# Products of alpha over four pairs of heads: one scan per direction instead of four, and no table A for the first five tiles

## The chip, the cores and the metric

The kernel runs on one core of a Trainium2 chip. The metric is the device time of one execution in microseconds; the median of several runs counts.

## The reference

Three layers follow one another; in what follows 4 batches, 8 heads, 768 positions and heads of 48 are meant.

```python
# 1. gated linear attention, position by position
state = alpha[:, :, t, :, None] * state + einsum('bhd,bhe->bhde', k[:, :, t], v[:, :, t])
y[:, :, t] = einsum('bhd,bhde->bhe', q[:, :, t], state)
# 2. x = y with the heads joined: 3072 rows of 384
xn = x / sqrt(mean(x*x) + 1e-6) * rms_g
x  = (silu(xn @ w_gate) * (xn @ w_val)) @ w_out          # 384 -> 1536 -> 384
# 3. each row to its best of 8 experts: relu(x @ w1[e]) @ w2[e], 384 -> 1024 -> 384,
#    times the gate's probability and a sigmoid of x @ w_output_gate[:, e]
```

The weights of layer 2 come as 64-bit numbers. alpha lies between 0.8 and 1.

## The kernel before

**Tiles.** The 3072 rows are 24 tiles of 128 positions of one batch; three tiles make a group of 384 rows, the unit of layer 2. The heads stand in four pairs (NP = 4): in a tile, the partitions hold the two heads of a pair (at 0 and at 64) and the free dimension holds pair and position, 4 x 128.

**Attention of a tile.** The step-by-step state becomes products of alpha within a tile. Z holds, for each position, the product of alpha over the positions after it; the product over the whole tile is `en`; A holds the product up to the position, divided by `en`. k is multiplied by Z, q by A; then the tile's scores, masked, and the state carried from the tile before give y. Z comes from `after_scan` (L269), a running product that goes backwards along the 127 positions of one pair, A from `upto_scan` (L283), a running product forwards over 128 positions that begins with the reciprocal of `en` (`ends`, L275). Both run on VectorE once per pair, so four times per tile. Their second operand is a column of ones that is broadcast.

**Two ways to bring in a tile.** Tiles 0 to 4 (`prework_nat`, L290) are loaded with positions on partitions and turned by TensorE (L246) into PSUM; the scans read alpha from PSUM, Z lies in a tile named aT, A in a tile named A, and q and k are multiplied on their way out of PSUM, or, by the letters in QM and KM, first copied out by ScalarE and then multiplied by VectorE (v) or GpSimd (p). Tiles 5 to 23 (`prework`, L330) are turned by VectorE (L342) from blocks of SBUF; alpha lies in aT, which the forward scan overwrites with A, and Z lies in a tile named A, of which there are two. Both multiplications (L371) run on VectorE in these tiles.

**Other work on the same engines.** Layer 2's weights arrive as pairs of 32-bit words; VectorE makes floats of them in three steps (L499, L502, L505) and ScalarE (L518) and VectorE or GpSimd (L509) split them in a high and a low part. Layer 2 is three matrix products per block of 128 hidden columns: ps_g and ps_v (L574), with ScalarE's L565 and L588 and VectorE's L566, L585 and L595 (GpSimd for some blocks of the first group) on what they leave in PSUM, and ps_o (L609). Layer 2 of one group runs while the attention of the next groups is prepared.

**What sets the order.** The program order comes from a list written by hand for the first three tiles (START), then from loops that give out one stage of attention or a few preparation steps per block of layer 2. From that order and its own idea of every instruction's cost a planner makes the order on each engine; it may move an instruction ahead of others. `pace` keeps the instructions whose names stand in K0, K1 or K2 in program order among themselves; the scans are named sc and the tile's number (sc0, sc1, sc4 and sc5 occur). SEATS names the PSUM bank of each early product. SIDE puts some tensors of tiles 1 and 2 where late weights will lie. Each engine works off its own queue in order.

Of the kernel before, what the change touches and what calls it, by code (L numbers as in the profile page):

```python
# [8 lines left out]
F32 = mybir.dt.float32  # L9
# [4 lines left out]
ALU = mybir.AluOpType  # L14
# [21 lines left out]
    'CR': [3, 3, 3, 2],  # L36
    'PRN': [1, 2, 1, 1],
    'JS': 6,
    'ABUF': 2,
    'ZBUF': 1,  # L40
    'IB': 0,
    'RA0': 2,
    'RB0': 13,
# [12 lines left out]
def gla_glu_moe_kernel(  # L56
# [16 lines left out]
    nc = tc.nc  # L73
    P = 128
    B, H, S, D = q.shape
    NT, DM = out.shape
    NP = H // 2
# [110 lines left out]
    for i in range(BS):  # L188
        t_ = att.tile([P, NP, 2 * D], F32, name=f"state{i}")
        nc.gpsimd.memset(t_, 0.0)  # L190
        state_of.append(t_)

    vt = {}
    pre = {}
    xT = {}
# [58 lines left out]
    def seat_of(t, nm, shape, bufs=1):  # L254
        if (t, nm) in SIDE:
# [7 lines left out]
    SIDE = {(2, "A"): ("wgle", 0), (2, "qT"): ("wgle", 1), (2, "kT"): ("wgle", 2),  # L263
            (1, "aT"): ("wvhe", 0), (1, "P0"): ("wvhe", 1), (1, "P1"): ("wvhe", 2),
            (1, "kn"): ("wghe", 0), (1, "xn"): ("wghe", 1), (2, "v"): ("wghe", 2)}

    def after_scan(Z, al, p):  # L269

        pace('sc' + str(now[0]), nc.vector.tensor_tensor_scan(out=Z[:, p, P - 2::-1], data0=al[:, p, P - 1:0:-1],
                                                data1=ones_f.to_broadcast([P, P - 1]),
                                                initial=1.0, op0=ALU.mult, op1=ALU.mult))

    def ends(t, Z, al):  # L275

        en = att.tile([P, NP, 1], F32, tag="en", name="en", bufs=4)
        rc = att.tile([P, NP, 1], F32, tag="rc", name="rc", bufs=2)
        pace('sc' + str(now[0]), nc.vector.tensor_tensor(out=en, in0=al[:, :, 0:1], in1=Z[:, :, 0:1], op=ALU.mult))
        pace('sc' + str(now[0]), nc.vector.reciprocal(out=rc, in_=en))  # L280
        return en, rc

    def upto_scan(A, al, rc, p):  # L283

        pace('sc' + str(now[0]), nc.vector.tensor_tensor_scan(out=A[:, p, :], data0=al[:, p, :], data1=ones_f.to_broadcast([P, P]),
                                                initial=rc[:, p, :], op0=ALU.mult, op1=ALU.mult))

    QM, KM, PM, XM, SM, HG, LV = (CFG[x] for x in ("QM", "KM", "PM", "XM", "SM", "HG", "LV"))

    def prework_nat(t):  # L290
        Z = seat_of(t, "aT", [P, NP, P], CFG["ZBUF"])
        A = seat_of(t, "A", [P, NP, P], CFG["ABUF"])
        qT = seat_of(t, "qT", [P, NP, P], 2)
        kT = seat_of(t, "kT", [P, NP, P], 2)
        nc.gpsimd.memset(Z[:, :, P - 1:P], 1.0)
        ps = {}

        def turn_a():
            now[0] = t
            ps[0] = turn_nat(t, 0)  # L300
            for p in range(NP):
                after_scan(Z, ps[0], p)
            en, ps["rc"] = ends(t, Z, ps[0])
            pre[t] = (en, qT, kT)

        def up():
            now[0] = t
            for p in range(NP):
                upto_scan(A, ps[0], ps["rc"], p)

        def turn(x, dst, by, mode):
            def go():
                ps[x] = turn_nat(t, x)
                if mode == "d":
                    pace(f'dm{t}', nc.vector.tensor_tensor(out=dst, in0=ps[x], in1=by, op=ALU.mult))
                else:
                    nc.scalar.activation(dst, ps[x], AF.Copy)
                    pace(f'qm{t}', (nc.gpsimd if mode == "p" else nc.vector).tensor_tensor(out=dst, in0=dst, in1=by, op=ALU.mult))
                if x == 2 and t + 1 == NAT:
                    load_tile(NAT)  # L320
            return go
        return {"a": turn_a, "r": up, "k": turn(1, kT, Z, KM[t]), "q": turn(2, qT, A, QM[t])}

    def load_v(t):
        b, c = place_of[t]
# [4 lines left out]
    def prework(t):  # L330
        if t < NAT:
# [1 line left out]
            for x in CFG['NO']:  # L333
                yield w[x]
            return
        aT = att.tile([P, NP, P], F32, tag="aT", name="aT", bufs=CFG["ZBUF"])
        Z = att.tile([P, NP, P], F32, tag="A", name="Z", bufs=CFG["ABUF"])
        qT = att.tile([P, NP, P], F32, tag="qT", name="qT", bufs=2)
        kT = att.tile([P, NP, P], F32, tag="kT", name="kT", bufs=2)

# [19 lines left out]
        def en():  # L360
            e_, ps["rc"] = ends(t, Z, aT)
            pre[t] = (e_, qT, kT)
        ps = {}
        yield en
        for p in range(0, NP, 2):
            def up(p=p):
                for pp in (p, p + 1):
                    upto_scan(aT, aT, ps["rc"], pp)
            yield up
# [949 lines left out]
```

## Time and profile before

| | |
|---|---|
| time, median of 3 runs | 900.53 us (900.36 to 902.38) |
| the profiled execution, its own time | 900.19 us |
| its span, first to last instruction | 898.5 us |
| TensorE busy with matmuls | 863.2 us (96% of the span) |
| VectorE busy | 579.6 us (65%) |
| ScalarE busy | 278.2 us (31%) |
| GpSimd busy | 197.3 us (22%) |
[...]

PE is TensorE, PEld its weight loads, DVE VectorE, ACT ScalarE, POOL GpSimd, SP the engine that issues most DMAs. A row of a timeline gives the start, the time to the end of the last of the merged instructions, the engine, the line, the operation, output and inputs with their shapes, and how many there are; in brackets is how long the engine had been idle and what ended that. The chain of waits follows the work back from the last instruction, at each step to what released it. [...] A busy TensorE is not one at full speed, since the ends of matmuls are modelled.

### The profile page before, as it was taken

How to read it: one execution, taken by the hardware profiler on the slowest of the kernel's cores; microseconds unless marked ns; L12 is line 12 of the kernel's file. 1: busy time of each engine (PE TensorE's matmuls, PEld its weight loads, DVE VectorE, ACT ScalarE, POOL GpSimd, SP SyncE). 2: the span in 40 equal slices, each digit the busy share in tenths (PEclk: the TensorE clock that was granted, in tenths of full speed). 3: DMA queues.
4: the chain of work that ended last, by engine and by line, in shares of the span. 5: the costliest groups of instructions: out<-in, count | busy, mean ns of one | idle time of the engine just before them, and what ended most of it. 6: DMA issues, size and time to landing. Idle time of an engine off the chain costs nothing.

```text
span 898.5 us, 15734 instructions
## 1 busy us (share of the span) xinstructions
PE 863.2 (96%) x6006; PEld 826.6 (92%) x6006; DVE 579.6 (65%) x1282; ACT 278.2 (31%) x575; POOL 197.3 (22%) x228
## 2 busy tenths in 40 slices
PE   7889899999999999999999999999999999999994
PEld 6778799999999999999999999999998999999994
DVE  7899969988986776777687774354444433443420
ACT  2333334322222222222222222224224443444431
POOL 4364512301010010010010001012124342343331
PEclk7796779999999999999999999999999999999998
DMA  9945894132332132232122100005044363266510
GB/s 194 199 130 140 216 292 137 41 74 60 84 100 53 47 85 52 65 85 57 50 68 57 43 11 28 1 14 171 1 167 150 111 206 117 81 194 194 169 44 26
DMA packets 117229, 90.14 MB, mean 100 GB/s; under 512 B 49051, under 2 KB 112284, under 8 KB 117152
## 3 DMA queue, kind: packets, MB, share of 16 engines
q1 hardware_dynamic: 112688, 79.64, 33.5%
q0 software_dynamic: 4464, 9.48, 3.1%
q8 instruction: 48, 0.79, 0.4%
q14 instruction: 29, 0.24, 0.1%
HBM read 73.29 MB, written 16.07 MB: 99 GB/s over the span
## 4 chain that ended last, share of the span: by engine, by line
PE 76%; DVE 10%; issue 5%; DMA 4%; POOL 2%; ACT 1%; SPq 1%; POOLq 0%; DVEq 0%; ACTq 0%
PE ps_g L574 16%; PE ps_v L574 15%; PE ps_o L609 15%; PE ps_b L1011 9%; PE ps_h L574 9%; PE ps_s L391 3%; DMA st<-in_moe_w_dram 3%; PE ps_y L430 3%; PE ps_y L426 2%; DVE F L502 1%; PE ps_k L415 1%; DVE F L505 1%; PE ps_st L456 1%; PE ps_x L480 1%; PE ps_t L975 1%
## 5 line engine op out<-in xcount | busy, mean ns | idle before, releaser
L565 ACT ACTIVATE tt<-ps_g 128x384 f32<-128x384 f32 x96 | 47.1, 491 | 178.9 <-PE ps_g L574 176.7
L588 ACT ACTIVATE hh<-tt 128x384 fp32r<-128x384 f32 x96 | 50.2, 523 | 160.5 <-DVE tt L585 160.3
L566 DVE SCALAR_TENSOR_TENSOR tt<-tt,ps_g 128x384 f32<-128x384 f32 x96 | 52.6, 548 | 73.1 <-ACT tt L565 72.6
L996 DVE SCALAR_TENSOR_TENSOR h<-ps_h,h 128x256 fp32r<-128x256 f32 (+6 forms) x72 | 38.0, 531 | 54.8 <-ACT h L995 54.7
L574 PE MATMUL ps_g<-xh,wgh 128*128 128x384 f32 x192 | 70.0, 365 | 2.9 <-ACT wgh L518 2.0
L574 PE MATMUL ps_v<-xh,wvh 128*128 128x384 f32 x192 | 68.5, 357 | 3.4 <-DVE tt L585 3.4
L1011 PE MATMUL ps_b<-w2a,h 128*128 128x384 f32 (+2 forms) x336 | 67.6, 340 | 2.8 <-ACT h L995 2.8
L574 PE MATMUL ps_g<-xl,wgh 128*128 128x384 f32 x192 | 67.1, 349 | 3.3 <-DVE xl L485 3.3
L609 PE MATMUL ps_o<-woh,hh 128*128 128x400 f32 x192 | 68.3, 361 | 0.0
L437 POOL TENSOR_SCALAR ss<-ss 128x1 f32<-128x1 f32 x24 | 5.4, 226 | 282.2 <-ACT xn L436 279.8
L609 PE MATMUL ps_o<-wol,hh 128*128 128x400 f32 x192 | 67.2, 350 | 0.0
L574 PE MATMUL ps_g<-xh,wgl 128*128 128x384 f32 x192 | 66.9, 348 | 0.0
L574 PE MATMUL ps_v<-xl,wvh 128*128 128x384 f32 x192 | 66.8, 348 | 0.0
L574 PE MATMUL ps_v<-xh,wvl 128*128 128x384 f32 x192 | 66.4, 346 | 0.0
L585 DVE SCALAR_TENSOR_TENSOR tt<-tt,ps_v 128x384 f32<-128x384 f32 x96 | 52.9, 551 | 20.4 <-PE ps_v L574 18.9
L1011 PE MATMUL ps_b<-w2b,h 128*114 128x384 f32 (+3 forms) x336 | 65.0, 338 | 0.2 <-ACT h L995 0.2
L609 PE MATMUL ps_o<-woh,hl 128*128 128x400 f32 x192 | 64.2, 352 | 0.0
L595 DVE TENSOR_TENSOR hl<-tt,hh 128x384 fp32r<-128x384 f32 x88 | 50.2, 570 | 19.1 <-ACT hh L588 18.9
L1011 PEld LDWEIGHTS ps_b<-w2a,h 128*128 128x128 f32 (+2 forms) x336 | 57.5, 181 | 4.3 <-ACT h L995 3.8
L1011 PEld LDWEIGHTS ps_b<-w2b,h 128*114 128x114 f32 (+3 forms) x336 | 57.4, 175 | 2.2 <-ACT h L995 0.6
L574 PE MATMUL ps_h<-x,w1b 128*128 128x456 f32 (+3 forms) x288 | 58.6, 344 | 0.0
L688 POOL DMA_INDIRECT bucket<-R,pos x24 | 24.3, 1011 | 145.4 <-issue 86.0
(249 smaller groups left out, 2100.0 us busy)
## 6 DMA issues: line engine op xcount, KB each, us to landing
st<-in_moe_w_dram SPq DMA_DIRECT2D x64, 384.0 KB, 4.6
bucket<-zrow SPq DMA_DIRECT2D x8, 772.0 KB, 11.9
stg<-in_moe_w_gate_dram SPq DMA_DIRECT2D x12, 384.0 KB, 3.8
stg<-in_moe_w_val_dram SPq DMA_DIRECT2D x12, 384.0 KB, 4.6
stg<-in_moe_w_out_dram SPq DMA_DIRECT2D x12, 384.0 KB, 4.2
v<-in_v_dram SPq DMA_DIRECT2D x23, 192.0 KB, 3.3
blk_a<-in_alpha_dram SPq DMA_DIRECT2D x38, 96.0 KB, 2.3
blk_q<-in_q_dram SPq DMA_DIRECT2D x38, 96.0 KB, 2.3
```

What stands on the lines that cost most here:

```text
L391: nc.tensor.matmul(ps[hh][:, p, :], lhsT=kT[r, p, :], rhs=qT[r, p, :], start=True, stop=True)
L430: nc.tensor.matmul(ps[u, h * D:h * D + D], lhsT=Pt[h % 2][:, h // 2, u], rhs=vt[t][:, h, :], start=first, stop=True, skip_group_check=True)
L565: nc.scalar.activation(tt, ps, AF.Tanh, scale=0.5)
L566: nc.vector.scalar_tensor_tensor(out=tt, in0=tt, scalar=1.0, in1=ps, op0=ALU.add, op1=ALU.mult)
L574: nc.tensor.matmul(ps, lhsT=a_[:, kc, :], rhs=b_[:, kc, :], start=(n == 0), stop=(n == 3 * KD - 1))
L585: nc.vector.scalar_tensor_tensor(out=tt, in0=tt, scalar=0.5, in1=ps, op0=ALU.mult, op1=ALU.mult)
L588: nc.scalar.activation(hh, tt, AF.Copy)
L595: eng.tensor_tensor(out=hl, in0=tt, in1=f(hh), op=ALU.subtract)
L609: nc.tensor.matmul(obank[s][i], lhsT=a_[:, sl], rhs=weight(b_, j), start=(j == j0 and n == 0), stop=(j == j1 - 1 and n == 2))
L688: nc.gpsimd.indirect_dma_start(out=bucket_of[g * GT + i], out_offset=OFF(ap=pos[:, i, 0:1], axis=0), in_=R[:, i, 0:RW], in_offset=None)
L996: nc.vector.scalar_tensor_tensor(out=hh[:, 1, :], in0=ps, scalar=0.0, in1=f(hh[:, 0, :]), op0=ALU.max, op1=ALU.subtract)
L1011: ins = nc.tensor.matmul(ob2[u][i][0:r], lhsT=hh[:, a_, sl], rhs=we[p][b_][:, j, :], start=(j == 0 and m == 0), stop=(j == KF2 - 1 and m = ...
```

## The change

- `after_scan` works on all four pairs at once, as one run of 511 elements: the first alpha of each pair is copied to `en` and then set to zero in place, and the second operand, now added and not multiplied, is a new table `begin`, zero but for a one at the first position of pairs 1 to 3. At a pair's border the running product is thereby reset to one. `en` is then multiplied by Z's first column.
- `upto_scan` is one run of 512 elements: the reciprocal of Z's first column goes to the first positions in `begin`, from which each pair starts.
- `begin` (128 x 4 x 128) is cleared once by GpSimd, before the loads' pads are set.
- In tiles 0 to 4 the forward scan writes into qT and q is multiplied in place from PSUM; A is gone, and for tile 0 the copy by ScalarE too (QM is gone). Z of tile 2 takes A's place in SIDE.
- In tiles 5 to 23 there is one Z and not two; GpSimd sets Z's last element in each tile; k is multiplied over all 128 positions; the preparation of a tile has 6 steps and not 9.

```diff
-    def after_scan(Z, al, p):
-        pace('sc' + str(now[0]), nc.vector.tensor_tensor_scan(out=Z[:, p, P - 2::-1], data0=al[:, p, P - 1:0:-1],
-                                                data1=ones_f.to_broadcast([P, P - 1]),
-                                                initial=1.0, op0=ALU.mult, op1=ALU.mult))
-    def ends(t, Z, al):
-        en = att.tile([P, NP, 1], F32, tag="en", name="en", bufs=4)
-        rc = att.tile([P, NP, 1], F32, tag="rc", name="rc", bufs=2)
-        pace('sc' + str(now[0]), nc.vector.tensor_tensor(out=en, in0=al[:, :, 0:1], in1=Z[:, :, 0:1], op=ALU.mult))
-        pace('sc' + str(now[0]), nc.vector.reciprocal(out=rc, in_=en))
-        return en, rc
-    def upto_scan(A, al, rc, p):
-        pace('sc' + str(now[0]), nc.vector.tensor_tensor_scan(out=A[:, p, :], data0=al[:, p, :], data1=ones_f.to_broadcast([P, P]),
-                                                initial=rc[:, p, :], op0=ALU.mult, op1=ALU.mult))
+    begin = att.tile([P, NP, P], F32, name="begin")
+    nc.gpsimd.memset(begin, 0.0)
...
+    def flat(x):
+        return x.rearrange("p a b -> p (a b)")
+    def after_scan(Z, al):
         en = att.tile([P, NP, 1], F32, tag="en", name="en", bufs=4)
+        W = NP * P
+        k_ = 'sc' + str(now[0])
+        pace(k_, nc.vector.tensor_copy(en, al[:, :, 0:1]))
+        pace(k_, nc.vector.memset(al[:, :, 0:1], 0.0))
+        pace(k_, nc.vector.memset(begin[:, 1:, 0:1], 1.0))
+        pace(k_, nc.vector.tensor_tensor_scan(out=flat(Z)[:, W - 2::-1], data0=flat(al)[:, W - 1:0:-1],
+                                              data1=flat(begin)[:, W - 1:0:-1], initial=1.0,
+                                              op0=ALU.mult, op1=ALU.add))
+        pace(k_, nc.vector.tensor_tensor(out=en, in0=en, in1=Z[:, :, 0:1], op=ALU.mult))
+        return en
+    def upto_scan(A, Z, al):
+        k_ = 'sc' + str(now[0])
+        pace(k_, nc.vector.reciprocal(out=begin[:, :, 0:1], in_=Z[:, :, 0:1]))
+        pace(k_, nc.vector.tensor_tensor_scan(out=flat(A), data0=flat(al), data1=flat(begin), initial=0.0,
+                                              op0=ALU.mult, op1=ALU.add))
...
     def prework_nat(t):
-        nc.gpsimd.memset(Z[:, :, P - 1:P], 1.0)
+        nc.gpsimd.memset(Z[:, NP - 1, P - 1:P], 1.0)
...
-            for p in range(NP):
-                upto_scan(A, ps[0], ps["rc"], p)
+            upto_scan(qT, Z, ps[0])
...
     def prework(t):
-        for p in range(0, NP, 2):
-            def sc(p=p):
-                for pp in (p, p + 1):
-                    after_scan(Z, aT, pp)
-            yield sc
...
+        def sc():
+            nc.gpsimd.memset(Z[:, NP - 1, P - 1:P], 1.0)
+            pre[t] = (after_scan(Z, aT), qT, kT)
+        yield sc
+        yield lambda: upto_scan(aT, Z, aT)
...
-        yield lambda: mul(t < LEAD and KM[t], kT[:, :, 0:P - 1], Z[:, :, 0:P - 1])
-        yield lambda: mul(t < LEAD and QM[t], qT, aT)
+        yield lambda: mul(t < LEAD and KM[t], kT, Z)
+        yield lambda: mul('d', qT, aT)
```

## Rows read from the trace of the kernel before

**Rows 1.** Busy by stretch: PE, PEld, DVE, ACT, POOL (instructions), PEclk, DMA share, GB/s.
```profile
43.00:95.00 52.00, 44.38 (x323) 39.94 (x322) 50.35 (x92) 17.03 (x41) 26.28 (x26) 0.86 0.53 139
95.00:123.00 28.00, 25.59 (x147) 24.44 (x147) 23.47 (x40) 10.10 (x25) 10.83 (x11) 0.63 0.91 250
123.00:167.00 44.00, 43.48 (x260) 42.97 (x258) 37.94 (x74) 18.20 (x41) 11.68 (x10) 1.00 0.55 154
167.00:600.00 433.00, 433.00 (x3318) 415.20 (x3319) 313.71 (x761) 105.50 (x238) 34.81 (x60) 1.00 0.21 54
```

**Rows 2.** Chain of waits by line, of 45 to 95 us and of 167 to 600 us.
```profile
by line: issue 17.7%; DVE F L502 10.3%; DVE F L499 8.6%; DVE aT L285 7.8%; DVE Fo L502 6.9%; DVE F L505 5.1%; DVE Z L271 4.9%; DVE aT L342 4.3%; DVE qT L342 4.0%; DVE tt L566 3.9%; DVE A L285 3.2%; DVE state L396 3.1%; DVE Fo L499 3.1%; DVE
by line: PE ps_o L609 27.8%; PE ps_g L574 27.5%; PE ps_v L574 27.2%; PE ps_s L391 4.8%; PE ps_y L430 4.7%; PE ps_y L426 3.3%; PE ps_st L456 1.6%; PE ps_k L415 1.4%; PE ps_x L480 1.4%; PE pc L538 0.1%; PE ps_r L670 0.1%; PE ps_r L671 0.1%; P
```

**Rows 3.** Timeline 0 to 14 us: start, length, engine, line, what, [idle before it <-releaser].
```profile
3.02 1.13 POOL L190 MEMSET state<- 128x384 f32 x3
4.35 1.12 PE L246 MATMUL ps_n<-ident,nat 128*128 128x128 f32 x4 [4.35 <-POOL nat L233]
5.51 1.36 DVE L271 TENSOR_TENSOR_SCAN aT<-ps_n,ones_f 128x127 f32<-128x127 f32 x4 [3.01 <-PE ps_n L246]
7.31 1.61 DVE L285 TENSOR_TENSOR_SCAN A<-ps_n,rc,ones_f 128x128 f32<-128x128 f32 x4
8.83 1.33 DVE L271 TENSOR_TENSOR_SCAN side<-ps_n,ones_f 128x127 f32<-128x127 f32 x4
11.47 1.16 PE L391 MATMUL ps_s<-qT,kT 48*128 48x128 f32 x8 [0.74 <-DVE kT L318]
```

**Rows 4.** Lines alone, whole run: duration ns min/median/max, first and last start us.
```profile
L271 DVE TENSOR_TENSOR_SCAN Z<-aT,ones_f x76: 374/393/1268, 68.9 to 532.2; 128x127 f32<-128x127 f32 x76
L285 DVE TENSOR_TENSOR_SCAN A<-ps_n,rc,ones_f x16: 456/459/484, 7.3 to 55.0; 128x128 f32<-128x128 f32 x16
L1114 DVE TENSOR_TENSOR_SCAN tab<-ones_f,tab x1: 176/176/176, 659.9 to 659.9; 128x8 f32<-128x8 f32 x1
L677 DVE COPY R<-tokid x8: 147/161/164, 195.6 to 650.1; 128x3 f32<-128x3 f32 x8
L1128 DVE MEMSET tab<- x1: 59/59/59, 171.7 to 171.7; 128x1 f32 x1
L182 DVE MEMSET blk_a<- x2: 112/112/112, 1.2 to 1.3; 32x64 f32 x2
```

**Rows 5.** Timelines of VectorE and GpSimd at two scans of tiles 5 and 6.
```profile
77.26 3.99 DVE L285 TENSOR_TENSOR_SCAN aT<-aT,rc,ones_f 128x128 f32<-128x128 f32 x4
77.52 1.02 POOL L509 TENSOR_TENSOR wgl<-F,wgh 128x384 fp32r<-128x384 f32 x1 [2.27 <-ACT wgh L518]
...
79.86 1.12 POOL L595 TENSOR_TENSOR hl<-tt,hh 128x384 fp32r<-128x384 f32 x1
...
94.52 3.97 DVE L285 TENSOR_TENSOR_SCAN aT<-aT,rc,ones_f 128x128 f32<-128x128 f32 x4
```

**Rows 6.** Timeline of TensorE, 92 to 134 us, where it waits for another engine.
```profile
94.75 0.44 PE L574 MATMUL ps_g<-xh,wgh 128*128 128x384 f32 x1 [1.97 <-ACT wgh L518]
...
113.32 0.87 PE L530 MATMUL pt<-ident,Fo 128*128 128x128 f32 x3 [2.41 <-DVE Fo L505]
```

**Rows 7.** Timeline of VectorE at 72 and at 104 us.
```profile
72.01 0.66 DVE L371 TENSOR_TENSOR kT<-kT,Z 128x508 f32<-128x508 f32 x1
...
104.27 1.11 DVE L342 STREAM_TRANSPOSE qT<-blk_q 128x512 f32<-128x512 f32 x1 [0.98 <-PE ps_y L426]
```

**Rows 8.** TensorE alone by stretch: busy (instructions), granted clock, DMA share, GB/s.
```profile
95.00:105.50 10.50, 10.50 (x63) 0.51 0.80 223
105.50:112.40 6.90, 5.41 (x56) 0.99 0.84 206
112.40:122.60 10.20, 9.28 (x32) 0.50 1.07 304
```

**Rows 9.** Timeline of GpSimd at 72 us.
```profile
72.13 1.45 POOL L509 TENSOR_TENSOR wol<-Fo,woh 128x400 fp32r<-128x400 f32 x1 [3.54 <-ACT woh L545]
```

More of the change, by code (lines that the diff above doesn't have):

```diff
@@ L38 @@
     'JS': 6,
-    'ABUF': 2,
-    'ZBUF': 1,
     'IB': 0,
@@ L261, in seat_of @@
         return att.tile(shape, F32, tag=nm, name=nm, bufs=bufs)
-    SIDE = {(2, "A"): ("wgle", 0), (2, "qT"): ("wgle", 1), (2, "kT"): ("wgle", 2),
+    SIDE = {(2, "aT"): ("wgle", 0), (2, "qT"): ("wgle", 1), (2, "kT"): ("wgle", 2),
             (1, "aT"): ("wvhe", 0), (1, "P0"): ("wvhe", 1), (1, "P1"): ("wvhe", 2),
             (1, "kn"): ("wghe", 0), (1, "xn"): ("wghe", 1), (2, "v"): ("wghe", 2)}
-    def after_scan(Z, al, p):
-        pace('sc' + str(now[0]), nc.vector.tensor_tensor_scan(out=Z[:, p, P - 2::-1], data0=al[:, p, P - 1:0:-1],
-                                                data1=ones_f.to_broadcast([P, P - 1]),
-                                                initial=1.0, op0=ALU.mult, op1=ALU.mult))
@@ L288, in gla_glu_moe_kernel @@
-    QM, KM, PM, XM, SM, HG, LV = (CFG[x] for x in ("QM", "KM", "PM", "XM", "SM", "HG", "LV"))
+    def flat(x):
+        return x.rearrange("p a b -> p (a b)")
+    def after_scan(Z, al):
+        en = att.tile([P, NP, 1], F32, tag="en", name="en", bufs=4)
+        W = NP * P
[8 more added lines that the diff above has]
+        return en
@@ L290, in prework_nat @@
+    def upto_scan(A, Z, al):
[3 more added lines that the diff above has]
+                                              op0=ALU.mult, op1=ALU.add))
+    KM, PM, XM, SM, HG, LV = (CFG[x] for x in ("KM", "PM", "XM", "SM", "HG", "LV"))
     def prework_nat(t):
-        Z = seat_of(t, "aT", [P, NP, P], CFG["ZBUF"])
-        A = seat_of(t, "A", [P, NP, P], CFG["ABUF"])
+        Z = seat_of(t, "aT", [P, NP, P])
@@ L300, in turn_a @@
             ps[0] = turn_nat(t, 0)
-            for p in range(NP):
-                after_scan(Z, ps[0], p)
-            en, ps["rc"] = ends(t, Z, ps[0])
-            pre[t] = (en, qT, kT)
+            pre[t] = (after_scan(Z, ps[0]), qT, kT)
         def up():
             now[0] = t
-            for p in range(NP):
-                upto_scan(A, ps[0], ps["rc"], p)
+            upto_scan(qT, Z, ps[0])
         def turn(x, dst, by, mode):
@@ L321, in turn @@
             return go
-        return {"a": turn_a, "r": up, "k": turn(1, kT, Z, KM[t]), "q": turn(2, qT, A, QM[t])}
+        return {"a": turn_a, "r": up, "k": turn(1, kT, Z, KM[t]), "q": turn(2, qT, qT, "d")}
     def load_v(t):
@@ L335, in prework @@
             return
-        aT = att.tile([P, NP, P], F32, tag="aT", name="aT", bufs=CFG["ZBUF"])
-        Z = att.tile([P, NP, P], F32, tag="A", name="Z", bufs=CFG["ABUF"])
+        aT = att.tile([P, NP, P], F32, tag="aT", name="aT", bufs=1)
+        Z = att.tile([P, NP, P], F32, tag="A", name="Z", bufs=1)
         qT = att.tile([P, NP, P], F32, tag="qT", name="qT", bufs=2)
@@ L353, in prework @@
         yield tr_qk
-        for p in range(0, NP, 2):
-            def sc(p=p):
-                for pp in (p, p + 1):
-                    after_scan(Z, aT, pp)
-            yield sc
[L360 to L369, printed above, removed]
+        def sc():
[3 more added lines that the diff above has]
+        yield lambda: upto_scan(aT, Z, aT)
         def mul(how, o, i):
             pace('km%d' % t, (nc.gpsimd if how == "p" else nc.vector).tensor_tensor(out=o, in0=o, in1=i, op=ALU.mult))
-        yield lambda: mul(t < LEAD and KM[t], kT[:, :, 0:P - 1], Z[:, :, 0:P - 1])
-        yield lambda: mul(t < LEAD and QM[t], qT, aT)
+        yield lambda: mul(t < LEAD and KM[t], kT, Z)
+        yield lambda: mul('d', qT, aT)
     def stages(t):
```

1 row of the table CFG is left out of this document.

## The prediction

> **What bounds the kernel now.** I read the busy time of each engine by stretch first, then the chain of waits of the same stretches, then the timelines where the two disagree with a simple picture. From 167 to 600 us TensorE is busy in all 433 us and the chain of waits is TensorE alone: not one line of VectorE stands in it [rows 1, 2]. From 123 to 167 us TensorE is busy in 43.5 of 44 us [rows 1]; a chain can be drawn through VectorE there, but nothing idles for it. So whatever the change does to the scans of tiles 7 to 23 is hidden, and what counts is how early TensorE comes to its unbroken work at about 123 us. From 43 to 95 us VectorE is busy in 50.4 of 52 us and the chain runs over its lines, the scans of tiles 4 to 6 among them [rows 1, 2]: here VectorE is the bound. At 94.75 us TensorE gets its weights and from then to 105.5 us works without a hole; at 104.27 us VectorE itself waits 0.98 us for TensorE; at 113.32 us TensorE waits once more, 2.41 us, for a weight that VectorE converts [rows 6 to 8]. [...] After 600 us come the experts, which the change doesn't touch; they shift with the rest.
>
> **A scan of 511 or 512 elements.** No such scan is in the trace. 127 elements take 0.393 us, 8 elements 0.176 us [rows 4], which is 1.82 ns per element: 0.393 + 384 x 0.00182 = 1.09 us. The other end comes from the distance of scans that follow one another: four of them, of 0.39 us each, end 1.36 us after the first began, so they start (1.36 - 0.39) / 3 = 0.32 us apart [rows 3]; if all of that were the price of elements, it would be 4 x 0.32 = 1.28 us. I take 1.18, the middle, since neither end is nearer to a long scan. The forward scans take 0.46 us each and start (1.61 - 0.46) / 3 = 0.38 us apart [rows 3, 4]; what they have over the others comes with their start from a column in memory, which the new scan, that starts from a constant, doesn't have.
> The rows put an element at 1.82 ns. [...]
>
> **What a tile gives back.** Before, a tile needs 1.36 us for the four backward scans and 1.61 for the forward ones and, with the product and the reciprocal between them, 8.83 - 5.51 = 3.32 us from its first scan to the next tile's [rows 3]. After: a copy of 4 elements (0.16, by the copy of 3 elements), two settings of 4 and 3 elements (between 0.06 and 0.11 each; I take 0.08), the backward scan 1.18, the product and the reciprocal as before but no longer one after the other (both read Z; 0.3 with their waits), the forward scan 1.10 until the next may start, and some 0.1 for waits of one on the other: 3.0 us. That is 0.3 to 0.4 us per tile, all of it in the forward half; Z itself is ready about 0.2 us later than before, since copy and settings stand ahead of it [rows 3, 4]. Tile 0's q is multiplied straight from PSUM; the same multiplication from SBUF took as long, so it gives nothing, and the ScalarE copy that goes was not waited for.
>
> **The start.** TensorE's first transpose waits for GpSimd's clearing of the pads, which stands behind the clearing of three states: 1.13 us for three times 384 columns, 0.36 apart [rows 3]. `begin` has 512 columns and stands between them: 0.36 x 512 / 384 = +0.48 us on the path. No cover is there; nothing if the loads land as late, which the row excludes by naming GpSimd. Tile 0 gives 0.3 back, but TensorE's first scores wait at 11.47 us for tile 0's k [rows 3], which needs Z of tile 0 and is multiplied after tile 1's Z: 0.48 - 0.33 + 0.2 = about +0.3 us there. From there TensorE and VectorE take turns until 43 us; I carry +0.3.
>
> **Tiles 3 to 6.** Tiles 3 and 4 read alpha from PSUM and gain 0.35 each: -0.7. In tiles 5 and 6 everything lies in SBUF, and the forward scans take 3.99 and 3.97 us where four undisturbed ones take 1.61 [rows 3, 5]: in the same time GpSimd works off three operations of about 1 us, and scans and operations take turns, each scan after the first lasting until the GpSimd operation is over. One scan gets in ahead of all three: 1.18 us instead of 3.99. But GpSimd's three operations are still to be done, and of VectorE's next four operations two (a conversion and a multiplication with both inputs in SBUF) will meet them. Each meeting costs up to 0.8 us, so I count 1.0 us for tile 5 and 1.4 us for tile 6, whose neighbours read PSUM, out of 2.8 each; the ends are 0.4 (all of it comes back) and 2.8 (none).
> That VectorE and GpSimd take turns is what the rows show. [...]
>
> **The sum.** To 94.75 us: +0.3 (start) - 0.7 (tiles 3, 4) - 1.0 (tile 5) = -1.4. Tile 6's 1.4 us come after TensorE has its weights; VectorE then waits for TensorE at 104.27 us anyway, so the gain only counts as far as conversions for the wait at 113.32 us move ahead of that: half, -0.7. Together -2.1 us, with ends of -0.8 (0.4 for tile 5, nothing for tile 6, start +0.48 more) and -4.5 (2.8 for tile 5, 1.4 for tile 6, less at the start). After 123 us: nothing. The profiled execution took 900.19 us, 0.34 less than the median of 900.53; on the median it is 900.5 - 2.1 = 898.4. I assume that the planner keeps the order on VectorE.
>
> **Rivals.**
> *TensorE's clock gives back more.* The stretch from 112.4 to 122.6 us at the lower level follows the hole of 2.41 us before 113.32 [rows 6, 8]. If VectorE's gain closes most of that hole, the level stays up, and 9.28 us of work take half: -4.6 on top, 893.8. For it: the hole is about as large as the gain. Against it: it ends with VectorE, and tile 6's share is uncertain.
> *The clock takes it back (slower).* [...] If TensorE gets its weights at 93.3 us but the following inputs don't move up with them, a hole opens there, the higher level doesn't come, and 5.41 us of work take twice that: +5.4 - 2.1 = +3.3, 903.8. It decides at any idle time of TensorE between 93 and 105 us; today there is none, and what is needed next comes from the same VectorE queue, which speaks against it.
> *The gain is hidden.* GpSimd now sets Z's last element in every tile from 5 on, and k's multiplication, in VectorE's queue, waits for that. At 72.13 us GpSimd's queue stands at an operation that waited 3.54 us for ScalarE and takes 1.45; k of tile 5 is multiplied at 72.01 [rows 7, 9]. If the setting falls behind that operation, VectorE stands until 73.6 us with all its conversions behind it: +1.6, so -0.5 in all, 900.0. It decides by whether the planner puts the setting before it; it has no inputs, which speaks for early.
> *The change doesn't do what it says.* If a scan of 512 elements costs four times one of 127 (4 x 0.393 = 1.57 us), a tile loses 0.5 us instead of gaining 0.3; tiles 3 to 6 then give -0.5 in all at best (one meeting with GpSimd instead of three), the start +0.9: about 900.9. The two lengths in rows 4 speak against it.
>
> **How the numbers follow.** About 0.3% (2.7 us) is what a measurement of this kernel can tell from no change. Forecast (896.0 to 899.7): 0.45, of which 0.20 lies below 897.8; higher clock 0.22; lower clock 0.17; hidden 0.11; scans not shorter 0.05. Faster: 0.20 + 0.22 = 0.42; slower: 0.17; within: 0.41. The range from 893.5 to 903.0 takes in all but half of the slower case and the tail of the clock's gain, less than 2 in 10.
>
> **What the profile after would show.** Right: scans of 1.1 to 1.3 us, two per tile; first transpose at 4.8 us; the forward scans of tiles 5 and 6 under 2 us, with conversions behind them that are longer than before; TensorE's unbroken work begins 1 to 4 us earlier; from there to the end the same length within 1 us. Wrong: idle time of TensorE between 167 and 600 us, another pattern of clock levels before 123 us, or an order on VectorE that isn't the old one with the scans merged. The last would make the whole sum void, since each wait then ends on something else.

## The result, and the profile after

The changed kernel is slower: 910.31 us against 900.44 us for the kernel before in the same comparison, a ratio of 1.0112 (95% interval 1.0091 to 1.0134). The forecast was 898.4 us with a range of 893.5 to 903.0; the time lies above the range, and none of the rivals reaches it. The profiled execution of the changed kernel took 909.88 us (span 908.2), 9.7 us more than that of the kernel before.

The busy time of each engine by stretch, of the changed kernel (columns: stretch, its length, PE, PEld, DVE, ACT, POOL, granted clock, DMA share, GB/s):

```profile
43.00:95.00 52.00, 46.12 (x324) 41.97 (x321) 50.34 (x87) 17.45 (x40) 29.66 (x26) 0.85 0.53 137
95.00:123.00 28.00, 24.94 (x184) 22.94 (x185) 26.42 (x46) 14.37 (x35) 12.49 (x13) 0.94 1.02 279
123.00:167.00 44.00, 39.67 (x224) 38.79 (x223) 34.75 (x70) 13.93 (x31) 10.19 (x11) 0.96 0.52 145
167.00:600.00 433.00, 433.00 (x3258) 410.69 (x3257) 298.73 (x680) 102.94 (x231) 36.44 (x75) 1.00 0.21 54
```

The granted clock is a share of full speed. In the traces of the kernel before and of the changed one it is 1.00 or 0.50 (half clock) at any time, and a figure between them is a mean over a stretch.

Beside [rows 1] two things stand out. From 95 to 123 us the clock is higher (0.94, it was 0.63), so the early part did become faster; from 123 to 167 us TensorE is busy in 39.67 us and no longer in 43.48. And from 167 to 600 us TensorE is still busy in every microsecond, yet shows fewer instructions: 3258, where it was 3318 (some records can be missing, so this is a hint only). A TensorE that is always busy has become slower. The chain of waits of that stretch, which ran over TensorE alone [rows 2], still does:

```profile
by line: PE ps_g L563 27.4%; PE ps_o L598 27.1%; PE ps_v L563 26.8%; PE ps_s L380 6.0%; PE ps_y L419 4.7%; PE ps_y L415 3.3%; PE ps_st L445 1.6%; PE ps_k L404 1.4%; PE ps_x L469 1.4%; PE pc L527 0.1%; PE ps_r L659 0.1%; PE ps_r L660 0.1%; P
```

One share has grown, that of the scores, `ps_s`: 6.0% and not 4.8% [rows 2], 1.2% of 433 us or 5.2 us.

To see where time goes along the run I use a milestone that both kernels have: the start of the j-th block of nine matmuls that write ps_g. The starts of some blocks in the two profiled executions, in us:

```
block                  0      3      5      9     12     15     20     30     50     70     95
before              35.1   60.9   94.8  134.0  149.8  166.9  201.1  264.5  384.8  504.4  641.0
after               44.2   69.9   95.3  128.1  148.3  166.6  203.4  268.0  391.4  513.9  650.7
after - before      +9.1   +9.0   +0.5   -6.0   -1.5   -0.3   +2.2   +3.6   +6.6   +9.5   +9.7
```

(Blocks 0 to 4 stand at other places in TensorE's order, so that they tell little.) Three phases follow: a gain of 6 us by block 9; its loss between block 9 and block 20, 8.2 us; and then a steady loss of 7.3 us up to block 70, while nothing idles. The times are of one execution of each kernel; what a second execution of the same kernel shows stands with the experiments.

**The steady loss.** The window from 250 to 520 us for the tile ps_s alone (same columns, without POOL; DVE is what reads it), first of the kernel before, then of the changed one:

```profile
250.00:520.00 270.00, 14.00 (x190) 11.52 (x186) 15.38 (x24) 0.00 (x0) 1.00 0.24 62
```
```profile
250.00:520.00 270.00, 18.32 (x176) 13.91 (x176) 14.44 (x23) 0.00 (x0) 1.00 0.24 62
```

Fewer matmuls, 4.3 us more. The timeline of TensorE shows why. The kernel before (start, us, engine, line, operation, output and inputs, how many):

```profile
293.33 0.34 PE L609 MATMUL ps_o<-wohe,hl 128*128 128x400 f32 x1
293.60 1.16 PE L391 MATMUL ps_s<-qT,kT 48*128 48x128 f32 x16
294.69 0.44 PE L574 MATMUL ps_g<-xh,wghe 128*128 128x384 f32 x1
```

The changed kernel:

```profile
291.75 0.49 PE L469 MATMUL ps_x<-ident,xn 128*128 128x128 f32 x3
292.17 0.71 PE L380 MATMUL ps_s<-qT,kT 48*128 48x128 f32 x6
292.81 0.45 PE L563 MATMUL ps_g<-xh,wghe 128*128 128x384 f32 x1
...
297.55 0.34 PE L598 MATMUL ps_o<-wohe,hl 128*128 128x400 f32 x1
297.82 0.93 PE L380 MATMUL ps_s<-qT,kT 48*128 48x128 f32 x10
298.69 0.45 PE L563 MATMUL ps_g<-xh,wghe 128*128 128x384 f32 x1
```

Before, a tile's 16 score matmuls follow one another: 294.69 - 293.60 = 1.09 us to the next matmul. After, six come directly behind ps_x and ten a block later: (292.81 - 292.17) + (298.69 - 297.82) = 0.64 + 0.87 = 1.51 us, 0.42 more for the same 16. ps_x takes 292.17 - 291.75 = 0.42 us to the matmul behind it; before, with ps_g behind it, it is 0.24 (288.37 to 288.61 us): another 0.18. Together 0.60 us for each tile, and a tile comes every 24 us: from block 24 (230 us) to block 70 (about 510 us) some 12 tiles, 7 us. That is the slope of the table. The planner had rearranged TensorE's instructions.

**The early part.** The merged scans cost what was forecast. Lines alone, by form, of the changed kernel (duration in ns: min/median/max, then first and last start):

```profile
L280 DVE TENSOR_TENSOR_SCAN Z<-aT,begin x19: 1210/1222/1895, 67.2 to 537.5; 128x511 f32<-128x511 f32 x19
L290 DVE TENSOR_TENSOR_SCAN aT<-aT,begin x19: 1214/1224/2105, 72.7 to 540.2; 128x512 f32<-128x512 f32 x19
L277 DVE COPY en<-aT x19: 131/163/978, 65.2 to 535.9; 128x4 f32<-128x4 f32 x19
```

The start, from the timeline of the changed kernel:

```profile
4.11 0.51 POOL L191 MEMSET begin<- 128x512 f32 x1
4.82 1.11 PE L245 MATMUL ps_n<-ident,nat 128*128 128x128 f32 x4 [4.82 <-POOL nat L232]
11.82 1.16 PE L380 MATMUL ps_s<-qT,kT 48*128 48x128 f32 x8 [0.80 <-DVE kT L318]
```

`begin` takes 0.51 us on GpSimd, the first transpose comes at 4.82 and not 4.35, and the first scores at 11.82 and not 11.47 us [rows 3]. Tile 5 on VectorE, where four forward scans had taken 3.99 us [rows 5]:

```profile
65.24 0.98 DVE L277 COPY en<-aT 128x4 f32<-128x4 f32 x1
...
72.67 2.05 DVE L290 TENSOR_TENSOR_SCAN aT<-aT,begin 128x512 f32<-128x512 f32 x1
74.65 1.35 DVE L488 TENSOR_SCALAR F<-stg 128x384 int32<-128x384 int32 x1
75.93 1.65 DVE L494 SCALAR_TENSOR_TENSOR Fo<-stg,Fo 128x384 int32<-128x384 int32 x1
...
83.23 1.90 DVE L280 TENSOR_TENSOR_SCAN Z<-aT,begin 128x511 f32<-128x511 f32 x1
...
88.39 2.10 DVE L290 TENSOR_TENSOR_SCAN aT<-aT,begin 128x512 f32<-128x512 f32 x1
```

One scan of 2.05 us, and the two conversions behind it last 1.35 and 1.65 us where undisturbed ones of the same lines last 0.35 and 0.54 us in the same timeline: what the scan no longer waits for GpSimd, they do (it saves 3.99 - 2.05 = 1.94 us, they lose 1.00 + 1.11 = 2.11). The last two rows are tile 6's scans. Its forward scan stands at 88.39 us, ahead of the wait for TensorE's weights; before it stood behind that, at 94.52 us against 94.75 for the weights [rows 5, 6]. So the order on VectorE changed as well. The waits of TensorE that had stood at 94.75 and 113.32 us [rows 6]:

```profile
95.26 0.44 PE L563 MATMUL ps_g<-xh,wgh 128*128 128x384 f32 x1 [1.38 <-ACT wgh L507]
...
110.99 0.55 PE L469 MATMUL ps_x<-ident,xn 128*128 128x128 f32 x3 [2.33 <-POOL xn L430]
...
135.62 0.44 PE L563 MATMUL ps_g<-xh,wgh 128*128 128x384 f32 x1 [2.58 <-DVE tt L555]
```

TensorE gets these weights no earlier than before (95.26 us, before 94.75). But the stretch at half clock behind them ends at 99.5 us (clock 0.62 from 95 to 99.5 us, 1.00 from 99.5 to 123), not at 105.5, and no second one comes before 123 us [rows 8]: the 6 us by block 9 are mostly clock. A new wait stands at 135.62 us. It is VectorE's, which in turn waited for a load of weights, for 5.02 us, and thereby held up the `tt` of L555 that stands behind the conversion:

```profile
134.15 0.36 DVE L488 TENSOR_SCALAR Fo<-stg 128x384 int32<-128x384 int32 x1 [5.02 <-DMA stg<-in_moe_w_out_dram]
```

After that idle time TensorE works at half clock from 137.0 to 140.4 us (granted clock 0.50). The chain of waits of 123 to 167 us now names this load first, with 32.2% (`DMA stg<-in_moe_w_out_dram`); for the kernel before no DMA is among the first twelve.

### The profile page after: what moved, and what is told of

It reads as the page before. It is cut to its first block, busy times and chain, and to the rows that moved or that the text cites. A ratio compares the mean times of both kernels' runs of the same rounds, so it can differ in the third digit from the quotient of the medians.

```text
span 908.2 us, 15687 instructions
## 1 busy us (share of the span) xinstructions
PE 870.5 (96%) x6006; PEld 826.9 (91%) x6006; DVE 570.2 (63%) x1210; ACT 278.0 (31%) x574; POOL 202.1 (22%) x248
## 4 chain that ended last, share of the span: by engine, by line
PE 74%; DVE 11%; DMA 6%; issue 5%; POOL 1%; ACT 1%; SPq 1%; POOLq 0%; DVEq 0%; ACTq 0%
PE ps_g L563 15%; PE ps_o L598 15%; PE ps_v L563 14%; PE ps_b L1000 9%; PE ps_h L563 9%; PE ps_s L380 4%; PE ps_y L419 3%; DMA st<-in_moe_w_dram 2%; DMA stg<-in_moe_w_out_dram 2%; PE ps_y L415 2%; DMA er<-bucket 1%; PE ps_k L404 1%; DVE F L494 1%; PE ps_st L445 1%; DVE F L491 1%
## 5 line engine op out<-in xcount | busy, mean ns | idle before, releaser
L555 DVE SCALAR_TENSOR_TENSOR tt<-tt,ps_g 128x384 f32<-128x384 f32 x96 | 52.9, 551 | 80.4 <-ACT tt L554 79.8
L563 PE MATMUL ps_h<-x,w1a 128*128 128x256 f32 (+3 forms) x288 | 53.6, 328 | 0.7 <-DVE h L985 0.7
```

The source lines that it names most:

```text
L555: nc.vector.scalar_tensor_tensor(out=tt, in0=tt, scalar=1.0, in1=ps, op0=ALU.add, op1=ALU.mult)
L563: nc.tensor.matmul(ps, lhsT=a_[:, kc, :], rhs=b_[:, kc, :], start=(n == 0), stop=(n == 3 * KD - 1))
```

## Experiments

In the diffs `-` is the changed kernel, or the kernel before where that is said. Times are medians; a ratio is to the kernel before in the same comparison, with its 95% interval.

### The scores kept whole: e1_pin, e4_pin_before

One instruction, the first score matmul of a tile, is kept in the order of the program; first in the changed kernel, then in the kernel before.

```diff
-                    nc.tensor.matmul(ps[hh][:, p, :], lhsT=kT[r, p, :], rhs=qT[r, p, :], start=True, stop=True)
+                    mm = nc.tensor.matmul(ps[hh][:, p, :], lhsT=kT[r, p, :], rhs=qT[r, p, :], start=True, stop=True)
+                    if not lead and p == 0 and hh == 0:
+                        tc.keep_in_program_order(mm)
```

> The kernel after, with one line more: from tile 6 on the first of a tile's 16 score matmuls is kept behind the TensorE instruction that stands before it in the program, so that the planner can't put the first six of them between two blocks of layer 2 and the rest a block later. Theory A (the loss is the split of the scores on TensorE, 0.41 us for the split and 0.17 us for the transposes that it now meets, in about 15 tiles): about 901 us, 9 below the kernel after, and the score group of a tile is again 16 matmuls in 1.09 us. Rival B (the loss comes from VectorE or GpSimd being later in each tile, and the split only shows it): the split goes but TensorE idles instead, about 910. Rival C (half and half): about 905.

> The kernel before with the same pin on the first score matmul. It has three tiles of eighteen with split scores, 0.4 us each. Theory A: 900.4 minus about 1.2, so 899. Rival (a pin by itself costs, since TensorE can no longer fill a wait with scores): 902 or more.

Measured: e1_pin 901.11 us (ratio 1.0011, 0.9993 to 1.0028), 9.2 us below the changed kernel; e4_pin_before 898.53 us (0.9980, 0.9958 to 1.0002). ps_s in e1_pin, from 250 to 520 us:

```profile
250.00:520.00 270.00, 12.78 (x176) 10.68 (x176) 15.47 (x24) 0.00 (x0) 1.00 0.25 62
```

As many matmuls as in the changed kernel, 12.78 us and not 18.32. From block 20 to block 70 e1_pin now takes 303.1 us; the kernel before takes 303.3, the changed one 310.5. So the steady loss is the order of the scores on TensorE. It isn't the scans.

### What splits the scores: e2_nine, e3_six

A tile's preparation is worked off in steps, some in every slot. The change cut them from nine to six. e2_nine gives the changed kernel three empty steps (first diff); e3_six gives the kernel before six steps, with its old scans (second diff, against the kernel before).

```diff
         yield sc
+        yield lambda: None
+        yield lambda: None
         yield lambda: upto_scan(aT, Z, aT)
+        yield lambda: None
```
```diff
-        for p in range(0, NP, 2):
-            def sc(p=p):
-                for pp in (p, p + 1):
-                    after_scan(Z, aT, pp)
-            yield sc
-        def en():
+        def sc():
+            for pp in range(NP):
+                after_scan(Z, aT, pp)
...
-        yield en
-        for p in range(0, NP, 2):
-            def up(p=p):
-                for pp in (p, p + 1):
-                    upto_scan(aT, aT, ps["rc"], pp)
-            yield up
+        yield sc
+        def up():
+            for pp in range(NP):
+                upto_scan(aT, aT, ps["rc"], pp)
+        yield up
```

> The kernel after, with the preparation of a tile from tile 5 on again in nine steps, three of them empty, so that every operation stands in the program order at the step it had before; the scans are the merged ones. Theory A1 (the merged steps moved the preparation ahead in the program order and this lets the planner split the scores): few splits, about 901 to 903. Rival A2 (the planner thinks the merged scans cheaper, and this lets it split): splits as in the kernel after, about 910.

> The kernel before, its scans one per pair as they were, but the preparation of a tile from tile 5 on in six steps as in the kernel after. Theory A1 (number of steps): the scores are split in most tiles and the time is about 909, with nothing of the scans changed. Rival A2 (cost of the scans in the planner): no splits, about 900.

Measured: e2_nine 901.82 us (1.0017, 0.9997 to 1.0036); e3_six 913.05 us (1.0146, 1.0110 to 1.0183). ps_s from 250 to 520 us, first in e2_nine, then in e3_six:

```profile
250.00:520.00 270.00, 13.26 (x176) 10.96 (x176) 15.38 (x24) 0.00 (x0) 1.00 0.25 62
```
```profile
250.00:520.00 270.00, 19.63 (x166) 15.42 (x166) 14.18 (x22) 0.00 (x0) 1.00 0.25 62
```

Empty steps take the split and the loss away: from block 20 to block 70 e2_nine takes 303.3 us, as the kernel before. Fewer steps alone make the kernel before slower than the changed one, without one merged scan; e3_six takes 312.2 us for the same blocks. Theory A1 is right for both. What splits the scores is the number of steps. The likely way is that another number shifts a tile's preparation against the slots, and with it where the planner puts the scores; no run shows the planner's own reckoning.

### Where the early gain goes: e5_bucket, e6_bucket_before

With the scores whole, the merged scans still gain nothing: 901.1 us against 898.5 with the old ones. The loss between block 9 and block 20 has to be explained. From 95 to 131 us the DMA engines are busy all the time (DMA share in e1_pin 1.06 from 95 to 123 us, 1.08 from 123 to 131); eight clearings of the bucket, 772 KB each, run beside the loads of weights. These two kernels ask for the clearings in stage 3 (e1_pin with that edit, and e4_pin_before with it).

```diff
-            if s == 2 and (n - CFG['IB']) % 2 == 0 and 0 <= (n - CFG['IB']) // 2 < E:
-                init_bucket((n - CFG['IB']) // 2)
+            if s == 3 and n < E:
+                init_bucket(n)
```

> The changed kernel with its scores kept whole (as e1_pin), and the eight clearings of the bucket (772 KB each) asked for in stage 3 instead of stage 2, so that they leave the SyncE queue behind the last loads of weights. Theory W: the lead that the merged scans bring by block 9 (e1_pin 4.8 us ahead of e4_pin_before there) is lost by block 11 because VectorE stands before the conversions of the expert weights, whose loads share the DMA engines with the clearings (DMA share about 1.0 from 95 to 131 us). Then here the weights land earlier, VectorE's idle stretch before 134 us is gone, a lead of 3 us or more stands at block 15, and the time is 896 to 898 us, 3 us or more below e1_pin's 901.1 and below e6_bucket_before. Theory C: the lead is lost to the order of the work on TensorE and to its clock, whatever the DMA engines do; then the idle stretch of TensorE before block 10 stays, the lead at block 11 is 1 us or less, and the time is 900 to 902 us.

> The kernel before with its scores kept whole (as e4_pin_before) and the clearings moved as in e5_bucket. Theory W: TensorE had no idle time from 123 to 167 us in the kernel before, so the DMA engines do not bound it there, and the time stays at 898.5 us within 1.5 us. Theory C: the same. A gain of 2 us or more would mean that the clearings cost the kernel before something too, in the stretch from 84 to 120 us, and then e5_bucket is to be read against this one only.

Measured: e5_bucket 900.22 us (0.9995, 0.9976 to 1.0013); e6_bucket_before 899.34 us (0.9994, 0.9977 to 1.0010). Theory W is right in its first step and wrong in the time. VectorE no longer waits for the load, TensorE works through to 140 us, and the lead over the kernel before is still 4.2 us at block 11 (e1_pin: 0.8). Most of that is the clearings' and not the scans': over e6_bucket_before, with the same clearings, the lead is 1.3 us at block 9 and 1.2 at block 11. At block 15 e5_bucket is 5.6 us behind it. The windows of e5_bucket (columns as above, with POOL):

```profile
123.00:140.00 17.00, 17.00 (x103) 16.65 (x102) 16.70 (x32) 6.17 (x15) 4.72 (x4) 1.00 0.52 154
140.00:170.00 30.00, 25.87 (x140) 24.74 (x140) 22.01 (x42) 8.58 (x20) 8.04 (x11) 0.83 0.14 41
```

and TensorE's longest wait in the second one:

```profile
155.57 0.69 PE L565 MATMUL ps_g<-xh,wgh 128*128 128x384 f32 x1 [2.38 <-DVE begin L279]
```

The DMA share falls to 0.52, VectorE becomes full (16.70 of 17 us), and from 146 us on TensorE waits for VectorE (0.85 us before 146.60, 0.89 before 152.03, 2.38 before 155.57) and works at half clock from 154.1 to 164.3 us (granted clock 0.50). One wait was taken away and another took its place. Theory C is right for the time; for block 11 it is wrong against the kernel before and nearly right against e6_bucket_before.

### The start: e7_start, e8_pin_start, e9_pin_before_b

`begin` is cleared behind the pads of the first block. e7_start does it on top of e5_bucket, e8_pin_start on top of e1_pin; e9_pin_before_b is e4_pin_before once more, beside e8_pin_start.

```diff
-    nc.gpsimd.memset(begin, 0.0)
...
         nc.gpsimd.memset(Z[:, NP - 1, P - 1:P], 1.0)
+        if t == 0:
+            nc.gpsimd.memset(begin, 0.0)
```

> As e5_bucket, and the clearing of the tile that holds the starts of the heads (0.51 us on GpSimd at 4.1 us, ahead of the pads of the first block) put behind those pads. Theory of the prediction: the first transpose waits for GpSimd, so the start comes back by 0.3 to 0.5 us (first transpose at 4.5 us or before, scores of tile 0 at 11.4 to 11.5 us), and the time falls by up to 0.5 us below e5_bucket. Rival: something else is late at the start, the scores of tile 0 stay at 11.8 us, and the time is that of e5_bucket.

> The changed kernel with its scores kept whole (as e1_pin) and `begin` cleared behind the pads of the first block (as e7_start), the clearings of the bucket where they were. Theory of the prediction, with its two mis-sized terms taken out: without the split scores (about 9 us) and without the late start (0.3 us at the first scores) the merged scans keep part of their lead, and the time is 1 us or more below e9_pin_before_b in the same call. Rival (the lead is given back): VectorE and the loads bound the stretch from 123 to 170 us, so that a lead there is worth nothing, and the time is that of e9_pin_before_b within 1.5 us.

> The kernel before with its scores kept whole, once more, beside e8_pin_start on the same chip. Both theories: 898 to 899 us, as in e4_pin_before (898.5).

Measured: e7_start 897.67 us (0.9979, 0.9960 to 0.9998); e8_pin_start 897.51 us (0.9983, 0.9968 to 0.9997); e9_pin_before_b 898.42 us (0.9988, 0.9971 to 1.0004). The first transposes in e7_start:

```profile
4.11 0.20 POOL L231 MEMSET nat<- 128x128 f32 x1
...
4.36 1.11 PE L244 MATMUL ps_n<-ident,nat 128*128 128x128 f32 x4 [4.36 <-POOL nat L231]
```

4.36 and not 4.82 us, and the first scores come at 11.55 us (changed kernel 11.82). The start was costed rightly. What it is worth at the end is not settled: e7_start lies 2.5 us below e5_bucket and e8_pin_start 3.6 us below e1_pin, more than the 0.3 us at the first scores, but the intervals of e5_bucket and e7_start overlap, and e1_pin and e8_pin_start were not compared on the same chip. Against e9_pin_before_b the merged scans gain 0.9 us, with overlapping intervals: no difference that is shown. These two kernels with `begin` late are the fastest measured here, 0.2% below the kernel before, and e4_pin_before, with the old scans, is as fast.

### Less work for VectorE: e10_lv, e11_lv_before

If VectorE's own work bounds the stretch from 140 us on, taking some of it away has to show. Four subtractions go to GpSimd, in e7_start and in e6_bucket_before.

```diff
-    'LV': (3, 20, 26, 25, 21, 35, 31, 22),
+    'LV': (3, 20, 21, 22),
```

> As e7_start (scores whole, clearings moved, `begin` cleared late), and four of the subtractions wvle/wole - weight minus its rounded part, 0.56 to 0.58 us each on VectorE between 127 and 165 us - go to GpSimd, which is busy for about 12 of the 47 us there. Theory V (once the loads are out of the way, VectorE's own work bounds 140 to 156 us, where e5_bucket shows it busy nearly without a gap and TensorE waiting 2.38 us at 155.57): the idle time of TensorE before 156 us shrinks by 1.5 us or more, the lead of 3 us at block 9 still stands at block 15, and the time falls by 1.5 to 2.5 us below e7_start's 897.7, to 895 to 896. Rival (turns with GpSimd): GpSimd takes 1.2 to 1.3 us for each, VectorE's operations with both inputs in SBUF wait for them, and the time stays within 1 us of e7_start's.

> As e6_bucket_before, with the same four subtractions on GpSimd. Theory V: the kernel before has more scan work on VectorE, so it gains as much or more, to 897 to 898 us (e6_bucket_before 899.3). Rival: no change, 899 to 900.

Measured: e10_lv 901.77 us (1.0034, 1.0013 to 1.0056), 4 us above e7_start; e11_lv_before 899.79 us (1.0005, 0.9987 to 1.0023), as e6_bucket_before. The intervals of e10_lv and e7_start don't overlap, so the edit made it slower. But it did not take work from VectorE. From 123 to 165 us (PE, PEld, DVE, ACT, POOL, then clock, DMA share, GB/s) e7_start, e10_lv and, with the old scans, e6_bucket_before:

```profile
123.00:165.00 42.00, 39.39 (x233) 38.31 (x233) 35.75 (x70) 15.61 (x37) 13.21 (x16) 0.96 0.28 84
```
```profile
123.00:165.00 42.00, 38.72 (x227) 37.00 (x227) 37.11 (x68) 15.14 (x37) 14.22 (x18) 0.96 0.28 84
```
```profile
123.00:165.00 42.00, 40.20 (x256) 39.62 (x255) 40.06 (x78) 16.91 (x39) 11.08 (x14) 1.00 0.31 91
```

VectorE is busy for 37.11 us and not 35.75 (with the old scans 40.17 in e11_lv_before and 40.06 in e6_bucket_before). A moved subtraction and the conversion beside it show why (e10_lv):

```profile
139.20 1.24 POOL L501 TENSOR_TENSOR wole<-Fo,wohe 128x400 fp32r<-128x400 f32 x1
139.45 1.20 DVE L491 TENSOR_SCALAR F<-stg 128x384 int32<-128x384 int32 x1
```

The conversion lasts 1.20 us, where an undisturbed one of that line lasts 0.35 (141.76 us), more than the 0.56 us that the subtraction had taken on VectorE. This is the rival's way, though its time, within 1 us of e7_start's, is missed too. So theory V was not tested by these runs: VectorE was never busy for less time. The wait of TensorE is still there in e10_lv:

```profile
159.20 0.69 PE L566 MATMUL ps_g<-xh,wgh 128*128 128x384 f32 x1 [2.13 <-DVE begin L278]
```

The row names the setting of `begin`, which TensorE doesn't read. VectorE's queue ahead of it points to the operation that TensorE needs: `tt` at L558, which reads a ps_g bank and ends just before, at 159.15 us (in the changed kernel the row at 135.62 us names its `tt`, L555, itself).

```profile
155.47 0.54 DVE L587 TENSOR_TENSOR hl<-tt,hh 128x384 fp32r<-128x384 f32 x1
155.94 0.15 DVE L282 TENSOR_TENSOR en<-en,Z 128x4 f32<-128x4 f32 x1
156.02 0.17 DVE L288 RECIPROCAL begin<-Z 128x4 f32<-128x4 f32 x1
156.13 0.72 DVE L388 TENSOR_TENSOR state<-state,en 48x192 f32<-48x192 f32 x2
156.88 1.23 DVE L289 TENSOR_TENSOR_SCAN aT<-aT,begin 128x512 f32<-128x512 f32 x1
158.02 0.67 DVE L361 TENSOR_TENSOR kT<-kT,Z 128x512 f32<-128x512 f32 x1
158.60 0.55 DVE L558 SCALAR_TENSOR_TENSOR tt<-tt,ps_g 128x384 f32<-128x384 f32 x1
159.10 0.06 DVE L278 MEMSET begin<- 128x3 f32 x1
```

Between `hl` at 155.47 and `tt` at 158.60 the second half of a tile's preparation and the state's product stand in one piece, 2.66 us, and TensorE's bank waits behind it. That speaks for the place in the queue and not the sum of VectorE's work; so does e6_bucket_before, whose VectorE is busy for 40.06 us, more than in e7_start, while its TensorE is held less. No run moves that piece alone, so the place is argued and not shown.

How general the loss is can be told from all kernels, by one execution of each: the time from the start of block 9 to that of block 20, the same 99 matmuls each of ps_g, ps_v and ps_o in all of them, in us, with TensorE's idle time in it.

```
old scans      before 67.1 (0.5)  e4 67.9 (1.4)  e6 68.2 (1.8)  e9 66.9 (0.7)  e11 69.4 (2.5)  e3 70.1 (2.8)
merged scans   after 75.3 (4.3)   e1 73.9 (4.4)  e2 72.0 (3.6)  e5 75.0 (4.1)  e7 70.9 (2.6)
               e8 71.3 (2.7)      e10 71.8 (3.3)
```

Every kernel with merged scans needs more than every one with the old scans: 71 to 75 us against 67 to 70. Between two executions of one kernel (e4 and e9) lies 1.0 us, and between the nearest two of the groups (e3 and e7) 0.8, so the difference of the groups is clear and that of a single pair need not be. Some of the rest over the idle time is half clock behind the waits (granted clock 0.50 for 3.4 us in the changed kernel, for 10.2 us in e5_bucket).

A lead of TensorE over the loads could be the reason. e9_pin_before_b was 5.9 us ahead of the kernel before at block 9 and still 6.1 us ahead at block 20. But its lead is there from the start (block 0 at 32.1 us, in the kernel before at 35.1, in e4_pin_before at 38.1; that execution, 892.9 us, was the fastest of its kernel). Its conversions come as much earlier too: the one that waits for a load in the changed kernel starts at 131.99 us, in the kernel before at 137.35. e7_start beside e6_bucket_before tells more, with the clearings moved in both. At block 9 it has no lead (130.9 us against 129.6), that conversion starts at 124.5 us in one and 124.4 in the other, in neither does VectorE wait for a load behind it, and e7_start still needs 70.9 us to block 20 where e6_bucket_before needs 68.2. So 2.7 us are lost there without a lead. Open is which of the merged kernels' differences does it: longer pieces that don't divide in VectorE's queue, one Z where there were two, or the places where the planner puts them. A second Z was not tried.

The gain ahead of block 9 isn't the merged scans' alone either. From block 5 to block 9 the four kernels with merged scans and the early clearing of `begin` need 32.8 to 33.0 us, the six executions with the old scans 35.4 to 39.3, and the three with merged scans and `begin` late 36.4 to 39.5. In these the half clock comes back ahead of block 9, in e7_start from 108.9 to 119.1 us (granted clock 0.50); from 95 to 123 us the clock is 0.82 in e7_start and e10_lv, where the changed kernel, e1_pin and e5_bucket have 0.94, and in e8_pin_start it is 0.81 from 112 to 123 us.

## Why the prediction was wrong

**Single operations: right.** A scan of 511 or 512 elements was put at 1.18 us and took 1.22. The forward scan, which now starts from a constant, takes as long as the backward one (1.224 and 1.222 us in the median); before, with its start from a column in memory, it took 0.459 us against 0.393 [rows 4]. A tile of 3.0 us: tile 0 took 3.02 (5.97 to 8.99 us, from its copy to the next tile's). First transpose at 4.8 us: 4.82. First scores +0.3 us: +0.35. Forward scans of tiles 5 and 6 under 2 us: 2.05 and 2.10, just missed. Conversions behind them longer: 1.35 and 1.65 us.

**A wait of the new copy: not counted, and there.** The price of a tile had 0.16 us for the new copy; in tile 5 it took 0.98 us, while its median is 0.163. The GpSimd operation beside it began earlier, at 64.97 us, and ended at 66.19; the copy ended at 66.22.

**The gain of the early part: right in sign, wrong in kind.** -2.1 us was the sum; by block 9 it was -6.0. The terms of VectorE were mis-sized. To TensorE's weights the forecast was -1.4 us, and they came 0.5 us later (95.26 against 94.75). Tile 5 was to keep 1.0 us and kept nothing (1.94 saved, 2.11 lost on the conversions behind). Tile 6's meetings with GpSimd, which the sum placed behind the weights, came ahead of them, since the order on VectorE wasn't the old one. The sum's mild end was added up wrongly besides: the terms that it names give between -0.3 and -0.6 and not -0.8. What brought the 6 us is the clock: the rival that TensorE's clock gives back more came true up to here, with another course. The half clock ended 6 us earlier and the second stretch of it didn't come, although a wait of 2.33 us still stood at 110.99.

The rival of the hidden gain didn't come true: GpSimd set Z for tiles 5 and 6 at 5.96 and 70.67 us, the latter just ahead of its operation of 1.26 us, and k of tile 5 was multiplied at 69.96 us. The reason that the prediction gave, that the setting has no inputs, doesn't hold: there is one Z, so the setting waits until k of the tile before is multiplied, and for 17 of the 19 settings GpSimd stood idle until such a product. Nor did the slower rival at its place: no run shows that idle time keeps the higher clock away there. TensorE idled for 1.38 us before 95.26 and for 0.46 us before 96.34, and the granted clock was 1.00 from 99.5 us on all the same.

**"After 123 us: nothing": this step failed, twice.** First, the unbroken work from 123 us on was taken as a property of TensorE, so that an earlier start would shift all that follows. What TensorE needs up to 167 us comes from VectorE, and that in turn from loads, and these had not moved by as much: the conversion that waits for its load starts at 134.15 us, 3.2 us earlier than in the kernel before (137.35), where TensorE was 6.0 us earlier. With the load out of the way, TensorE waited for VectorE's queue. Why the merged kernels need longer there even without a lead stays open. Rows 1 showed a DMA share of 0.91 from 95 to 123 us and of 0.55 behind it, and the prediction didn't ask whether the loads would come earlier too. Of the 6 us nothing was left at block 15.

Second, and larger, the price of the steady part. The prediction looked for idle time of TensorE there; none came. It assumed "that the planner keeps the order on VectorE" and named another order as what "would make the whole sum void", but only for VectorE, and it gave this neither a price nor a chance. VectorE's order did change, in tile 6; the one that cost most was TensorE's, and the edit that changed it stood in the list of the change: six steps and not nine. It was costed at nothing, as bookkeeping. e1_pin puts it at 9.2 us (910.3 - 901.1), e3_six, with the old scans, at 12.8 us (913.05 against 900.21 for the kernel before beside it).

**The scans' own worth.** With the scores whole and the start mended, the merged scans give 0.9 us or nothing (e8_pin_start against e9_pin_before_b). The forecast of 2.1 us for them would have been inside the error of such a comparison, but its reason, that what is won before 123 us stays won, doesn't hold for them. e1_pin, with `begin` cleared early, even lies 2.6 us above e4_pin_before.

## What to carry to other kernels

Where a planner interleaves streams by steps, the number of steps is part of the schedule: a change that merges steps should be costed for the order of every engine, the saturated one above all, and empty steps or one pinned instruction tell the two effects apart. A saturated engine can lose without idling (here TensorE, 7.3 us between block 20 and block 70), so compare the time of equal work there (a group's start to the next start) and not the busy share. A lead that is won ahead of a stretch in which two engines and the loads are nearly in balance is to be measured at its far end: here it lasted where VectorE's work and the loads came earlier by as much (e9_pin_before_b), and the merged kernels lose time there even without a lead (e7_start beside e6_bucket_before).

## What the runs showed of the hardware

- Breaking a group of small matmuls cost TensorE time (kernel before against the changed one). Sixteen score matmuls (48 rows, 128 columns) take 1.09 us in one group, and 0.64 + 0.87 us as six and ten between wide matmuls: 0.42 us for one more group, about nine times what one of these matmuls adds within a group ((1.09 - 0.64) / 10 = 0.045 us). Three transposes (ps_x) took 0.42 us with a score matmul behind them and 0.24 us with a wide one.
- A VectorE copy of four elements, 0.163 us in the median, took 0.98 us beside a GpSimd operation of 1.22 us (changed kernel), and a product of four elements up to 1.01 us (in e1_pin, at 162.0 us).
- A subtraction of 0.56 us that went from VectorE to GpSimd lengthened the VectorE conversion beside it from 0.35 to 1.20 us (e10_lv).
- The clearing of 512 columns took 0.51 us on GpSimd; a setting of four elements on VectorE took 0.06 us.
